# The loads of raw q and k go from SP's queue to GpSimd's in a fused attention and two-MoE kernel

## The chip, the cores and the metric

One core of a Trainium2 chip runs the whole program. The metric is the device time of one execution in microseconds (us), the median of several runs. Engines are named as in the profile: PE (TensorE), DVE (VectorE), ACT (ScalarE), POOL (GpSimd), SP (SyncE, which only issues DMAs here).

## The reference

Causal attention with a bias from a running sum, then two dense two-layer blocks on its output, all in float32:

```python
scores = scale * np.matmul(q, k.transpose(0, 1, 3, 2))        # B, H, S, D = 4, 8, 576, 64
cum = np.cumsum(np.maximum(s, 0.0), axis=-1)
bias = -(cum[:, :, :, None] - cum[:, :, None, :])
scores = np.where(causal, -1000000000.0, scores + np.minimum(bias, 0.0))
attn = softmax(scores)
x = np.matmul(attn, v)                                         # then [2304, 512]
h = np.maximum(x @ w_in, 0.0);  x = h * h @ w_out              # d_ff = 2048
h = x @ w_in2;                  out = h * np.cos(h) @ w_out2
```

## The kernel before, in words

**Work.** The 2304 tokens are cut into nine blocks of 256. `_units` lists 96 "heads": each is one head of one batch over a run of query rows (256, 192, 128 or 64 of them) of one block. A head is done in steps of up to 128 query rows, one "job" each; heads 24 to 31, 56 to 63 and 80 to 95 have one job, the others two. While the attention of later blocks runs, the first MoE block (lines 850 to 902: `g1`, `gact`, `grest`, `g2`) is done for earlier ones: each `step` (line 996) issues a part of the attention pipeline and one or more slots of 12 matmuls of `g1` (L857) or `g2` (L886). After about 535 us the attention is over; the rest of the first MoE block and then the second one (L1246, L1301) remain.

**One head, from 16 on.** `load_raw` (line 210) brings q and k transposed, 128 partitions by 448 to 768 floats, into a tile `raw` that has two buffers. `prep_high` (L347, L348 on ACT) casts it to float32r, `prep_low` (L355, L358 on DVE) subtracts and keeps the rest in the tiles `hi` and `k2`; L358 is the last reader of `raw`, so the load of head n+2 may start when L358 of head n has ended. `load_ext` (L340, issued by POOL) puts four rows of bias terms into `k2`; the buffer it writes is free when the last QK matmul (L502) of head n-2 has read it. Then come QK on PE (L502), mask and minimum on DVE (L516), exp on ACT (L533), two splits on DVE (L561, L565), a DMA transpose of the result issued by SP (L571), and PV on PE (L602). Where a job's width is no multiple of 128, POOL first clears the padding of the tile `p` (L560), and L561 of that job waits for it.

**Order of the work around the change.** Every engine and queue runs its instructions strictly in program order. In a head's first step, `heads_ahead` issues `load_ext` of the next head at the step's start, `prep_high` and `prep_low` of the next head in its middle, and at its very end `load_raw` of the head three further on:

```python
heads_ahead(i, (next_, load_ext, 2))
...
heads_ahead(i, (nhigh, prep_high, 2))
...
heads_ahead(i, (nlow, prep_low, 2))
...
heads_ahead(i, (nraw, load_raw, 4))
```

SP's queue holds, beside the raw loads, the weight loads (L179), the transposes (L571), the loads of prepared v (L368) and its stores (L433), and the stores of block results (L895). POOL's queue holds the ext loads (L340), the loads of v (L380) and the clearing of padding (L560).

Of the kernel before, what the change touches and what calls it, by code (L numbers as in the profile page):

```python
# [24 lines left out]
BT = 256  # L25
# [90 lines left out]
def attention_moe_moe_kernel(  # L116
# [18 lines left out]
    nc = tc.nc  # L135
# [74 lines left out]
    def load_raw(n):  # L210
        nq, nl = heads[n][6], heads[n][8]
        if n < H:
            return
        if n < EARLY:
            t = at.tile([128, KQ], F32, tag=("hi", "k2")[n % 2], bufs=2, name="early1")
            nc.sync.dma_start(out=t[0:64, 0:2 * BT], in_=qk[n, 0:64, 0:2 * BT])
            nc.sync.dma_start(out=t[64:66, 0:2 * BT], in_=c1_d[n - H])
            hd[n] = t
            return
        raw = at.tile([128, KQ], F32, tag="raw", bufs=2, name="raw")  # L220
        nc.sync.dma_start(out=raw[:, BT - nq:BT + nl], in_=qk[n, :, BT - nq:BT + nl])
        hd[n] = [None, None, raw]

    def v_own(b):
# [29 lines left out]
    def store_ones(eng, n0, n1):  # L254
# [10 lines left out]
        out=mask[:, 512:640], in_=mask[:, 512:640], pattern=[[-1, 128]], compare_op=ALU.is_ge,  # L265
# [4 lines left out]
        out=ident, in_=ident, pattern=[[-1, 128]], compare_op=ALU.not_equal, fill=1.0,  # L270
# [3 lines left out]
    for t in early[2:]:  # L274
        early_ones(t, nc.gpsimd)
    nc.vector.tensor_scalar(
        out=cs[0:32, 0:S], in0=cs[0:32, 0:S], scalar1=0.0, scalar2=8.0, op0=ALU.max, op1=ALU.mult
    )
    cc = []
    for x0, x1, t in ((0, BT, "xh"), (BT, S, "xl")):  # L280
        nc.vector.tensor_tensor_scan(
            out=c8[0:32, x0:x1], data0=cs[0:32, x0:x1], data1=cs[0:32, x0:x1],
# [713 lines left out]
    def step(moe=0, bits=0, attn=True):  # L996
# [52 lines left out]
        if attn:  # L1049
            heads_ahead(i, (nraw, load_raw, 4))  # L1050
# [104 lines left out]
    for k in range(NB1):  # L1155
# [8 lines left out]
        for i in range(J):  # L1164
# [24 lines left out]
            n = len(slots) - last - nslots + math.ceil(nslots * (i + 1) / J)  # L1189
# [233 lines left out]
```

## Time and profile before

| what | value |
|---|---|
| median of 3 runs | 1001.28 us (999.33 to 1001.86) |
| the profiled execution, its own time | 998.74 us |
| span of the profiled execution | 997.0 us |
| busy, share of the span | PE 96%, PEld 74%, DVE 73%, ACT 66%, POOL 16% |
| granted TensorE clock | 1.0 throughout |
| DMA queue of SP and ACT (q1) | 119.05 MB, 46.4% of 16 engines' span |
| DMA queue of POOL (q0) | 6.29 MB, 2.4% |

Busy shares are averages over stages with different limits. A busy PE is no PE at its peak, since matmuls overlap in the records; what counts is where PE stands idle and what ended the idle time. DMA issues are not counted as busy. The views used below are: the table of stretches, the chain of work that ended last, the waits (who waited for whom), the timeline, and the view of one line or tile.

### The profile page before, as it was taken

Reading aid. Unit: us, or ns where it says so; the run is one execution under the profiler, and the core shown is the slowest. Engines: PE = TensorE matmul, PEld = TensorE weight load, DVE = VectorE, ACT = ScalarE, POOL = GpSimd, SP = SyncE. Lnnn points to the kernel's source line nnn. Section 1 sums busy time; section 2 is a strip of 40 time slices with the busy share of each in tenths; the row PEclk is TensorE's granted clock in tenths of the full one; section 3 lists DMA queues with packets and bytes.
Section 4 is the critical chain, followed back from the end, with each engine's and each line's share of the span. In section 5 each row is a group of like instructions: output and inputs, shape, how many; then the busy total and the mean of one; then the engine's idle time right before and its main releaser. Section 6 shows DMA issues by size and latency. Waiting matters only on the chain.

```text
span 997.0 us, 20518 instructions
## 1 busy us (share of the span) xinstructions
PE 961.9 (96%) x7266; PEld 738.4 (74%) x7266; DVE 723.6 (73%) x1865; ACT 654.6 (66%) x1596; POOL 162.3 (16%) x258
## 2 busy tenths in 40 slices
PE   5999899999999999999999999999999999999998
PEld 4798898899999998999999997444544454444444
DVE  6879788878778897777987267798987545545555
ACT  5789776778778777676776587777865443433433
POOL 2000011111111111111210022430043340001101
PEclk9999999999999999999999999999999999999999
DMA  8955589756897876477898579110000000011001
GB/s 275 296 175 181 145 198 197 163 131 161 178 180 168 182 192 150 118 147 164 189 214 167 194 260 354 62 40 1 1 1 1 0 1 1 3 40 43 27 17 64
DMA packets 150711, 126.65 MB, mean 127 GB/s; under 512 B 108048, under 2 KB 125792, under 8 KB 150608
## 3 DMA queue, kind: packets, MB, share of 16 engines
q1 hardware_dynamic: 146688, 119.05, 46.4%
q0 software_dynamic: 3904, 6.29, 2.4%
q8 instruction: 57, 0.93, 0.4%
q14 instruction: 46, 0.38, 0.1%
q10 hardware_dynamic: 16, 0.01, 0.0%
HBM read 85.25 MB, written 15.81 MB: 101 GB/s over the span
## 4 chain that ended last, share of the span: by engine, by line
PE 81%; DVE 10%; ACT 5%; issue 2%; DMA 2%; SPq 0%; DVEq 0%; ACTq 0%
PE hps L857 19%; PE y L886 18%; PE o L1301 17%; PE hp L1246 17%; PE qkp L502 4%; PE pvs L602 4%; DVE wt L750 1%; DVE st L729 1%; DVE sb L516 1%; DMA raw<-in_qk_dram 1%; PE xps L657 1%; DVE wt L753 1%; PE qkp L493 1%; ACT st L719 1%; ACT sb L533 1%
## 5 line engine op out<-in xcount | busy, mean ns | idle before, releaser
L857 PE MATMUL hps<-xh,wt 128*128 128x256 f32 x1152 | 239.8, 291 | 4.2 <-ACT g L868 4.1
L886 PE MATMUL y<-gh,wt 128*128 128x256 f32 x1152 | 236.7, 289 | 0.0
L857 PEld LDWEIGHTS hps<-xh,wt 128*128 128x128 f32 x1152 | 190.3, 192 | 6.9 <-ACT g L868 5.8
L886 PEld LDWEIGHTS y<-gh,wt 128*128 128x128 f32 x1152 | 188.9, 191 | 1.2
L1246 PE MATMUL hp<-yh,wt 128*128 128x512 f16 (+1 forms) x640 | 185.9, 358 | 0.0
L1301 PE MATMUL o<-wt,gh 128*128 128x512 f16 x576 | 171.3, 379 | 2.0 <-ACT wt L1316 1.9
L886 PE MATMUL y<-gl,wt 128*128 128x256 f32 x576 | 163.0, 283 | 2.7 <-DVE gl L876 2.7
L857 PE MATMUL hps<-xl,wt 128*128 128x256 f32 x576 | 163.6, 284 | 0.9 <-DVE xl L674 0.9
L1246 PEld LDWEIGHTS <-wt 128*128 128x128 f16 x960 | 92.2, 98 | 93.3
L1258 ACT ACTIVATE a<-hp,hsc 128x512 f32<-128x512 f32 (+1 forms) x80 | 51.4, 643 | 118.2 <-PE hp L1246 116.8
L868 ACT ACTIVATE g<-hps 128x256 f32<-128x256 f32 x144 | 54.6, 379 | 106.4 <-PE hps L857 104.8
L1246 PE MATMUL hp<-yl,wt 128*128 128x512 f16 (+1 forms) x320 | 114.4, 358 | 0.0
L886 PEld LDWEIGHTS y<-gl,wt 128*128 128x128 f32 x576 | 110.1, 191 | 3.7 <-DVE gl L876 3.1
L857 PEld LDWEIGHTS hps<-xl,wt 128*128 128x128 f32 x576 | 111.0, 193 | 1.4 <-DVE xl L674 1.1
L1301 PE MATMUL o<-wt,gl 128*128 128x512 f16 x288 | 109.2, 379 | 0.4 <-DVE gl L1288 0.4
L1259 DVE TENSOR_SCALAR kf<-a 128x512 f32<-128x512 f32 (+1 forms) x80 | 33.6, 420 | 103.7 <-ACT a L1258 103.3
L1301 PEld LDWEIGHTS <-gh 128*128 128x128 f16 x576 | 56.2, 98 | 66.7 <-issue 2.4
L533 ACT ACTIVATE sb<-sb,nb 128x128 f32<-128x128 f32 (+8 forms) x160 | 93.7, 586 | 11.8 <-DVE nb L516 11.5
L340 POOL DMA_DIRECT2D k<-ext_d x80 | 40.9, 511 | 336.2 <-ACT g L869 94.9
L516 DVE CUSTOM_DVE_ANT_0 sb<-qkp,mask 128x128 f32<-128x128 f32 (+8 forms) x160 | 72.6, 454 | 12.5 <-PE qkp L493 5.5
L1267 ACT ACTIVATE a<-kf 128x512 f32<-128x512 f32 (+1 forms) x80 | 46.8, 585 | 46.9 <-DVE kf L1260 46.4
L876 DVE TENSOR_TENSOR gl<-g,gh 128x256 fp32r<-128x256 f32 x144 | 60.0, 417 | 21.5 <-PE y L886 10.4
(119 smaller groups left out, 1690.3 us busy)
## 6 DMA issues: line engine op xcount, KB each, us to landing
rw<-in_w_dram SPq DMA_DIRECT2D x64, 512.0 KB
raw<-in_qk_dram SPq DMA_DIRECT2D x32, 352.0 KB
raw<-in_qk_dram SPq DMA_DIRECT2D x16, 384.0 KB
v_d<-vt SPq DMA_DIRECT2D x16, 320.0 KB
raw<-in_qk_dram SPq DMA_DIRECT2D x16, 320.0 KB
vb<-v_d SPq DMA_DIRECT2D x32, 160.0 KB
vr<-in_v_dram POOLq DMA_DIRECT2D x15, 320.0 KB, 4.4
y_d<-yst SPq DMA_DIRECT2D x18, 256.0 KB
```

The costliest lines, as they stand in the source:

```text
L340: nc.gpsimd.dma_start(out=hd[n][1][64:68, BT - nq:BT + nl], in_=ext_d[n, :, BT - nq:BT + nl])
L502: nc.tensor.matmul(p[0:r, 0:cn], m[0:kk, qo:qo + r], m[0:kk, BT + c0:BT + c0 + cn], start=(kk == 128), stop=(kk == 68),)
L516: nc.vector.tensor_tensor_reduce(out=sb[0:r, c0:c0 + cn], in0=p[0:r, 0:cn], in1=mask[0:r, mo + c0:mo + c0 + cn], scale=-0.125, scalar=(3.0 ...
L533: nc.scalar.activation(out=sb[0:r, 0:w], in_=sb[0:r, 0:w], func=ACTF.Exp, scale=-1.0, bias=j["nb"], accum_out=pd[n - h % 2]["z"][0:r, ti, ...
L857: nc.tensor.matmul(hp, w[:, a, c * 128:(c + 1) * 128], (xh, xl)[e][:, c, :], start=(n == 0), stop=(n == 3 * KD - 1),)
L868: nc.scalar.activation(out=g, in_=hp, func=ACTF.Relu)
L876: nc.vector.tensor_tensor(out=gl, in0=g, in1=gh, op=ALU.subtract)
L886: nc.tensor.matmul(yps[k][d // 2][:, d % 2, :], w[:, a, d * 128:(d + 1) * 128], (gh, gl)[e], start=(f == 0 and n == 0 and d % 2 == 0), sto ...
L1246: nc.tensor.matmul(hp, w[:, a, c * 128:(c + 1) * 128], (yh, yl)[e][:, c, :], start=(m == 0), stop=(m == 3 * KD - 1),)
L1258: nc.scalar.activation(out=a, in_=hp, func=ACTF.Copy, scale=sm["hsc"][:, j, f:f + 1], bias=0.25)
L1267: nc.scalar.activation(out=a, in_=kf, func=ACTF.Sin, scale=-6.2831850)
L1301: nc.tensor.matmul(ops[j][a], (gh, gl)[e][:, a * 128:(a + 1) * 128], w[:, x, :], start=(first and m == 0), stop=(last and m == 2),)
```

## The change

The 80 loads of `raw` (heads 16 to 95) are issued by GpSimd instead of SP. Nothing else is changed; the loads of heads 8 to 15 (lines 216, 217) stay on SP.

```diff
         raw = at.tile([128, KQ], F32, tag="raw", bufs=2, name="raw")
-        nc.sync.dma_start(out=raw[:, BT - nq:BT + nl], in_=qk[n, :, BT - nq:BT + nl])
+        nc.gpsimd.dma_start(out=raw[:, BT - nq:BT + nl], in_=qk[n, :, BT - nq:BT + nl])
         hd[n] = [None, None, raw]
```

POOL, in the last stretch of one-job heads (`k_` with a number is the tile of one ext load; the first row is the ext load of head 90, the fourth that of head 91):

```order
 L340 DMA k_8593<-ext_d 4x704
 L560 MEMSET p 128x2x64
+L221 DMA raw<-in_qk_dram 128x704
 L340 DMA k_8673<-ext_d 4x704
 L560 MEMSET p 128x2x64
```

Between an ext load with its clearing and the next such pair there now stands one raw load: that of head 92 stands ahead of the ext load of head 91.

SP in the same stretch, before and then now:

```order
L221 DMA raw<-in_qk_dram 128x704
L571 DMA_TRANSPOSE pt<-p 128x10x128
L895 DMA y_d<-yst 128x512 x2
L368 DMA vb<-v_d 128x640
L221 DMA raw<-in_qk_dram 128x704
```

```order
L368 DMA vb<-v_d 128x640
L571 DMA_TRANSPOSE pt<-p 128x10x128
L895 DMA y_d<-yst 128x512 x2
L368 DMA vb<-v_d 128x640
L571 DMA_TRANSPOSE pt<-p 128x10x128
```

The raw load has left its place behind a transpose, two stores of block results and a load of v; nothing else on SP changed its order.

POOL at the program's start (`early` are tiles of the first heads, `vr` holds v):

```order
 L191 MEMSET early 2x2x256
 L192 MEMSET early 2x2x256
+L221 DMA raw<-in_qk_dram 128x768
 L380 DMA vr<-in_v_dram 128x2x320
+L221 DMA raw<-in_qk_dram 128x768
```

The first raw load (head 16) now follows the clearing at the start directly, ahead of POOL's first load of v; its buffer has no earlier user.

## Rows read from the trace of the kernel before

**Rows 1.** The page: busy time by engine, and the chain by engine.
```profile
PE 961.9 (96%) x7266; PEld 738.4 (74%) x7266; DVE 723.6 (73%) x1865; ACT 654.6 (66%) x1596; POOL 162.3 (16%) x258
...
PE 81%; DVE 10%; ACT 5%; issue 2%; DMA 2%; SPq 0%; DVEq 0%; ACTq 0%
```

**Rows 2.** Stretches: length, busy PE, PEld, DVE, ACT, POOL, clock, DMA share, GB/s.
```profile
0.00:40.00 40.00, 29.06 (x111) 24.12 (x112) 31.42 (x96) 24.43 (x68) 5.95 (x15) 1.00 0.87 285
...
165.00:210.00 45.00, 40.54 (x408) 36.79 (x408) 35.27 (x117) 30.94 (x92) 8.39 (x20) 1.00 0.75 177
...
500.00:535.00 35.00, 33.61 (x359) 32.93 (x358) 30.81 (x88) 25.16 (x65) 5.44 (x16) 1.00 0.90 204
```

**Rows 3.** Chain in order of time (start, length, what): its pieces on raw.
```profile
166.74 4.20 DMA raw<-in_qk_dram
...
512.06 4.26 DMA raw<-in_qk_dram
```

**Rows 4.** Waits, 78 to 540 us: who waited for whom; total us, times, longest.
```profile
ACT hi L347 <- DMA raw<-in_qk_dram: 15.6, 12, 4.6
...
DVE hi L355 <- ACT hi L347: 5.7, 12, 1.2
...
DVE p L561 <- POOL p L560: 8.4, 10, 1.1
...
PE hps L857 <- ACT g L868: 2.9, 5, 1.0
...
PE qkp L502 <- DVE hi L355: 0.7, 1, 0.7
```

**Rows 5.** Timeline around the raw load of head 91: start, length, what, [idle before].
```profile
507.34 0.75 DVE L358 TENSOR_TENSOR k<-raw,hi 64x576 fp32r<-64x576 f32 x1
...
508.48 1.94 SPq L571 DMA_TRANSPOSE pt<-p  x1
...
510.47 1.05 SPq L895 DMA_DIRECT2D y_d<-yst  x2
...
512.06 0.43 SPq L221 DMA_DIRECT2D raw<-in_qk_dram  x1
...
516.40 0.78 ACT L347 CAST hi<-raw 128x704 fp32r<-128x704 f32 x1 [2.03 <-DMA raw<-in_qk_dram]
...
517.71 0.38 PE L857 MATMUL hps<-xh,wt 128*128 128x256 f32 x1 [0.72 <-ACT g L868]
```

**Rows 6.** View of L340: issue (ns min/median/max) and landing of the ext loads.
```profile
L340 POOL DMA_DIRECT2D k<-ext_d x80: 502/508/729, 75.7 to 528.5; - x80
...
DMA to landing us min/median/max: 1.8/3.2/5.9
```

**Rows 7.** View of L380: landing of POOL's loads of v.
```profile
DMA to landing us min/median/max: 3.3/4.4/6.4
```

**Rows 8.** Timeline around the ext load of head 91, POOL, DVE and PE.
```profile
510.97 0.50 POOL L340 DMA_DIRECT2D k<-ext_d  x1 [3.22 <-DVE p L561]
...
511.46 0.22 POOL L560 MEMSET p<- 128x128 f16 x1
...
512.58 0.75 DVE L358 TENSOR_TENSOR k<-raw,hi 64x576 fp32r<-64x576 f32 x1
...
514.46 0.46 DVE L561 TENSOR_SCALAR p<-sb 128x576 f16<-128x576 f32 x1
...
519.37 0.29 PE L502 MATMUL qkp<-k 68*128 68x288 f32 x1
```

**Rows 9.** Timeline of POOL at the start: its first load of v.
```profile
74.46 0.76 POOL L380 DMA_DIRECT2D vr<-in_v_dram  x1 [67.73 <-ACT wt L738]
```

**Rows 10.** Timeline: L561 beside a load that POOL issues, and alone.
```profile
164.99 0.75 POOL L380 DMA_DIRECT2D vr<-in_v_dram  x1 [2.68 <-PE qkp L502]
...
165.35 0.64 DVE L561 TENSOR_SCALAR p<-sb 64x576 f16<-64x576 f32 x1
...
169.44 0.45 DVE L561 TENSOR_SCALAR p<-sb 64x576 f16<-64x576 f32 x1
```

## The prediction

> **What bounds the kernel now.** I read the page first. PE is busy for 96% of the span and holds 81% of the chain [rows 1]; the time can only fall where PE stands idle or waits. The table of stretches then says where the moved loads matter. They lie between 78 and 540 us, and the two stretches with most of PE's trouble there are 165 to 210, with 40.54 busy of 45, and 500 to 535, with 33.61 of 35 [rows 2]. In both, heads have a single job, so a raw load is due every four to five microseconds. DVE is close behind PE there: 30.81 of 35. The clock is 1.00 throughout, so it is no part of the sum.
>
> Next the chain in order of time, because a wait counts only if it is on it. Raw loads are on it twice, for 4.20 and 4.26 us, in just these two stretches [rows 3]. The waits say how much arrives at PE. ACT waits for raw 12 times, 15.6 us in all; DVE waits behind that cast for 5.7 us; but PE's own idle time behind ACT's L868 is 2.9 us and behind DVE's L355 it is 0.7 us [rows 4]. Most of ACT's waiting is slack that PE never sees.
>
> The timeline shows why a load is late. L358 of head 89 starts at 507.34, takes 0.75 and so frees the buffer at 508.09. SP is then at a transpose (508.48, 1.94 us) and two stores (510.47, 1.05), and issues the load at 512.06, 3.97 us after it could have. ACT gets the data at 516.40, 4.34 us after the issue, having been idle for 2.03; PE loses 0.72 just after [rows 5]. The load itself is not slow, its place in the queue is.
>
> **The change part by part.** It removes 80 DMAs from SP, adds 80 to POOL, and moves each past other work on both.
>
> *Earlier issue.* On POOL, a raw load stands behind an ext load and a clearing that were released before L358 ended, so it goes at 508.1 instead of 512.1. Its landing from POOL's queue is not in the trace. From below it is bounded by the ext loads, median 3.2 us [rows 6], from above by the slowest load of v, 6.4; I take the median of the loads of v, 4.4 [rows 7], since those are 320 KB and a raw load is 352 in this stretch. That gives 512.5. ACT was ready at 516.40 - 2.03 = 514.37, so this wait goes, and it nearly goes even at 6.4 (514.5). What PE can win is its idle time behind these waits, 2.9 + 0.7 = 3.6 us at most [rows 4], and nothing at least, if another wait is due at once. DVE is next there: it has 35 - 30.81 = 4.2 us of idle time in 35. I take -2.5 us, two thirds, because the five waits behind L868 are not all behind a raw load.
>
> *The ext load, now behind the raw load.* Each raw load stands ahead of the next head's ext load and waits for DVE. Before, the ext load of head 91 went at 510.97; the L358 of head 90 that the raw load ahead of it needs ends at 512.58 + 0.75 = 513.33 [rows 8]. Add the raw load's own issue, which lies between 0.51 for 4 rows [rows 6] and 0.75 for a load of v [rows 10]; I take 0.75, the nearer in size. So the ext load goes at 514.1, 3.1 us later than before. With its median of 3.2 us it lands at 517.3, and if it can't land before the raw load ahead of it in the same queue, at 513.33 + 4.4 = 517.7. QK needs it at 519.37 [rows 8]. That is 1.7 us of cover; at the slowest landing, 5.9 [rows 6], it would be 0.6 late. I take +0.3 us in all. One late landing in ten of the 32 one-job heads would be 3 x 0.6 = 1.8, which is the bound. Heads with two jobs have a whole further step between the raw load and the next ext load; there I take nothing.
>
> *The clearing, now behind both.* The clearing after the ext load then ends at 514.08 + 0.50 + 0.22 = 514.80, while the L561 that needs it ran at 514.46 [rows 8]: 0.34 us of new waiting on DVE. It comes in every second one-job head, since after each pair DVE has the division of the pair's output between, which covers it: 16 x 0.34 = 5.4 us of DVE time. Such waits exist already, 8.4 us of them [rows 4], and PE is busy all the same. What hides them is DVE's idle time, 4.2 in 35, about 0.5 us a head, more than 0.34 in every second one. I take +0.6, with 0 and 5.4 as bounds.
>
> *The start.* POOL does nothing from 74.46 - 67.73 = 6.73 us until its load of v [rows 9]. The raw load of head 16 has nothing to wait for and so is issued at 6.7 instead of 78. In the first 40 us the DMA engines are 87% busy and move 285 GB/s [rows 2]; 128 x 768 x 4 bytes = 393 KB at that rate take 1.4 us. If weights and first heads come later by all of it, that is +1.4; if the remaining 13% take it, nothing. I take +0.4.
>
> *DVE beside POOL's issues.* L561 took 0.64 us beside a load issued by POOL and 0.45 without one [rows 10]. A raw load's issue starts where L358 ends and is over 0.75 later, while the next L561 comes 514.46 - 513.33 = 1.13 after it [rows 8]. I take 0; if every load hit such an instruction, it would be 80 x 0.19 = 15 us of DVE time, hidden in part. The trace shows how weakly the other side is disturbed: 80 ext loads took 502 to 729 ns to issue, with a median of 508, while DVE was busy for 73% of the span [rows 6, 1].
>
> *SP.* It loses 80 issues and what they waited for. Its transposes still wait for their own inputs and for free buffers; I take 0, and no loss, since none of its work is put behind anything new.
>
> **Sum.** -2.5 + 0.3 + 0.6 + 0.4 + 0 + 0 = -1.2 us against the profiled execution's 998.74, that is 997.5. The median of the runs shown, 1001.28, is 2.5 above that execution, so on its scale the forecast is **1000.1 us**. A measurement of this kernel can tell about 0.3%, 3 us, from no change; the forecast is no measurable difference.
>
> **Rivals.**
>
> *A: the raw waits were worth more than PE's idle time shows.* For it: the chain holds 8.46 us of raw loads [rows 3], and ACT and DVE wait 15.6 and 5.7 us [rows 4]; freed, they run ahead and take other small waits from PE. Against it: PE is 96% busy, and its recorded idle time behind these waits is 3.6. If half of the 8.46 comes out and nothing is given back, the time is about 997; if all does, 993.
>
> *B: POOL's line becomes the loop, and it is slower.* L358 of one head, then the raw load's issue, the ext load's, the clearing, L561, and from there DVE's work up to the next L358. Place: the 32 one-job heads. Price: 5.4 us of clearing, 1.8 of ext loads, 1.4 at the start, with 0.5 of the gain left, so +8.1 and 1009 in full, 1005 when half of it gets through. It decides where DVE's idle time, 0.5 us a head, no longer covers the wait: at a raw issue of about 1.4 us instead of 0.75. For it: DVE is at 88% in that stretch. Against it: the gain removes DVE's own 5.7 us of waiting behind the cast, which is as much as the clearing costs.
>
> *C: DVE holds up POOL's issues.* As a mechanism here: a raw issue that has to sit out one DVE instruction of 0.75 us [rows 8] makes the load, the ext load and the clearing behind it that much later: 32 x 0.75 = 24 us of further DVE waiting, of which 32 x 0.5 = 16 is covered, so some +8 on top of B, 1015. The Trainium skill, page "SBUF — State Buffer", section "SBUF: two separate sides", states it as a rule against this change: a DMA issued from GpSimd has its descriptors written through a port that some VectorE instructions hold for themselves, and the page's advice is to issue from SP or ACT. By its figure (section "A bandwidth-pool intuition that's wrong", 3100 ns against 620) an estimate is 2.5 us more for each load. The trace doesn't bear it out: no ext load took over 729 ns to issue [rows 6].
>
> That the loads are not moved is excluded: the order shows all 80 on POOL.
>
> **Chances.** Forecast 0.49; A 0.23; B 0.24; C 0.04. Faster by over 0.3% (under 998.3) is A, 0.23; within 0.3%, 0.49; slower (over 1004.3) is B and C, 0.28. **Range** 996.0 to 1006.5: downwards the full 3.6 and the runs' own spread (999.33 to 1001.86), which leaves out the last tenth with A's 993; upwards most of B, leaving out its full price and C.
>
> **What would show it.** Right: ACT's wait for raw falls from 15.6 us to under 5; raw loads go within 0.3 us of L358's end; POOL's landing of raw is 4 to 5 us; the chain has no raw in it; waits of L561 for L560 grow by several us; PE's busy share stays near 96%. Wrong: PE waits for an ext load at L502 (B by the ext load), DVE's idle time in 500 to 535 used up and PE's busy time there below 33 (B by the clearing), or raw issues of over 1 us on POOL (C). If PE's waits behind L868 and L355 go and the time falls by more than 3 us, the sum undervalued the chain (A).

## The result and the profile after

The changed kernel takes **1010.49 us** (median of 6 runs, 1008.17 to 1016.9) against 1000.49 (6 runs, 998.35 to 1001.86) for the kernel before on the same chip: ratio 1.0111, 95% interval 1.0081 to 1.0141. It is slower; the forecast was 1000.1 and no difference, the range ended at 1006.5. The profiled execution is the slowest of the six, 1016.9 us, with a span of 1015.1; another profile of the same kernel, called `again` below, has 1008.39 and 1006.6.

The page of the profile after, busy time and DMA queues, against [rows 1]:

```profile
PE 969.0 (95%) x7266; PEld 745.6 (73%) x7266; DVE 723.9 (71%) x1865; ACT 655.4 (65%) x1596; POOL 211.1 (21%) x338
...
q1 hardware_dynamic: 135168, 92.31, 37.3%
q0 software_dynamic: 10048, 33.03, 12.0%
```

The loads went where the change says: 26.7 MB have moved from SP's queue to POOL's, and DVE and ACT are as busy as before. The stretches, against [rows 2]:

```profile
0.00:40.00 40.00, 27.29 (x104) 22.53 (x104) 29.65 (x91) 23.40 (x64) 6.46 (x16) 1.00 0.88 286
165.00:210.00 45.00, 40.60 (x409) 37.95 (x410) 36.18 (x116) 31.53 (x92) 13.46 (x31) 0.96 0.73 168
310.00:360.00 50.00, 46.41 (x462) 45.19 (x460) 39.63 (x107) 37.16 (x100) 9.61 (x17) 0.99 0.98 176
...
500.00:535.00 35.00, 31.44 (x328) 30.64 (x327) 28.77 (x80) 25.48 (x64) 9.95 (x23) 1.00 0.93 202
```

In the last stretch of one-job heads PE has lost 2.17 us of 35 (33.61 to 31.44), and DVE has lost 2.04 too: it is not DVE that has become the bound, both wait. (The kernel is some 14 us behind by then, so this window holds earlier heads of the same stretch than it did before.) The clock column is the second thing to see: 0.96 and 0.99, where the kernel before had 1.00. The waits from 78 to 560 us (the last L502 now stands at 554.8, before at 536.1), against [rows 4]:

```profile
DVE p L561 <- POOL p L560: 11.5, 15, 1.3
...
ACT hi L347 <- DMA raw<-in_qk_dram: 11.0, 8, 2.1
...
PE qkp L502 <- DMA k<-ext_d: 9.3, 6, 3.9
...
DVE hi L355 <- ACT hi L347: 3.9, 9, 1.2
...
PE hps L857 <- ACT g L868: 0.5, 1, 0.5
```

ACT's waits behind raw fell from 15.6 to 11.0 us, and PE's own wait behind L868 went from 2.9 to 0.5. One wait is new, and it is PE's: L502 for the ext load. The views of L340 and L221 tell how late these loads are, against [rows 6] (this profile tells the landing of 73 of the 80 ext loads and 69 of the 80 raw loads):

```profile
L340 POOL DMA_DIRECT2D k<-ext_d x80: 521/522/817, 78.4 to 543.1; - x80
DMA to landing us min/median/max: 1.9/3.8/8.1
```

```profile
L221 POOL DMA_DIRECT2D raw<-in_qk_dram x80: 548/565/605, 6.7 to 541.1; - x80
DMA to landing us min/median/max: 3.0/4.1/9.5
```

A raw load now goes 0.55 us after the end of L358 in one-job heads (median; before 1.92), and the ext load behind it 1.11 us after, where it went 1.85 us ahead of that end before: it is 3 us later.

How one such load stops PE is seen in `again` at head 58, the third of the second one-job stretch. First the kernel before, the ext load of that head and the first matmul that needs it:

```profile
344.57 0.52 POOL L340 DMA_DIRECT2D k<-ext_d  x1 [0.70 <-PE qkp L502]
...
351.31 0.30 PE L502 MATMUL qkp<-k 68*64 68x288 f32 x1
```

And `again`, the timeline of the same head:

```profile
345.66 0.75 DVE L358 TENSOR_TENSOR k<-raw,hi 64x576 fp32r<-64x576 f32 x1
...
346.96 0.56 POOL L221 DMA_DIRECT2D raw<-in_qk_dram  x1 [2.67 <-ACT g L868]
...
347.52 0.52 POOL L340 DMA_DIRECT2D k<-ext_d  x1
...
351.65 0.30 PE L502 MATMUL qkp<-hi 128*64 128x288 f32 x1
...
355.20 0.47 PE L502 MATMUL qkp<-k 68*64 68x288 f32 x1 [3.25 <-ACT k L348]
```

The raw load of head 59 waits for L358 of head 57 (end at 346.41), the ext load of head 58 stands behind it and lands 7.54 us after its issue, at 355.06; 0.14 us later PE goes on, after 3.25 us of idle time. (The row puts the wait down to L348; that of head 58 had ended at 348.97.) The raw load of head 59, just ahead in the queue, took 7.32 us to land itself. The clock falls at 354.02, while PE still stands, and PE, busy for most of the next stretch, works at half speed (the column after the busy times is the granted clock; 0.50 is the 1.2 GHz level):

```profile
354.10:360.80 6.70, 5.60 (x34) 5.54 (x35) 1.86 (x6) 2.86 (x8) 1.29 (x3) 0.50 0.49 126
```

### The profile page after: what moved, and what is told of

Same layout as the page of the kernel before. It is cut to its first block, busy times and chain, and to the rows that moved or that the text cites. A ratio compares the mean times of both kernels' runs of the same rounds, so it can differ in the third digit from the quotient of the medians.

```text
span 1015.1 us, 20456 instructions
## 1 busy us (share of the span) xinstructions
PE 969.0 (95%) x7266; PEld 745.6 (73%) x7266; DVE 723.9 (71%) x1865; ACT 655.4 (65%) x1596; POOL 211.1 (21%) x338
## 4 chain that ended last, share of the span: by engine, by line
PE 42%; DVE 4%; ACT 2%; issue 1%; DMA 1%; DVEq 0%; POOL 0%; ACTq 0%; POOLq 0%
PE o L1301 17%; PE hp L1246 16%; PE y L886 4%; PE hps L857 4%; DMA k<-ext_d 1%; DMA raw<-in_qk_dram 1%; PE pvs L602 1%; ACT wt L744 0%; DVE kf L1260 0%; DVE wt L753 0%; DVE a L1273 0%; PE qkp L502 0%; DVE wsc L783 0%; DVE kf L1259 0%; ACT a L1258 0%
## 5 line engine op out<-in xcount | busy, mean ns | idle before, releaser
L886 PE MATMUL y<-gh,wt 128*128 128x256 f32 x1152 | 239.5, 291 | 0.0
L857 PEld LDWEIGHTS hps<-xh,wt 128*128 128x128 f32 x1152 | 192.4, 194 | 3.5 <-ACT g L868 2.4
L886 PEld LDWEIGHTS y<-gh,wt 128*128 128x128 f32 x1152 | 191.2, 193 | 1.2
L868 ACT ACTIVATE g<-hps 128x256 f32<-128x256 f32 x144 | 54.6, 380 | 124.6 <-PE hps L857 123.1
L221 POOL DMA_DIRECT2D raw<-in_qk_dram x80 | 45.4, 568 | 285.0 <-ACT gh L870 89.1
L561 DVE TENSOR_SCALAR p<-sb 128x512 f16<-128x512 f32 (+7 forms) x128 | 46.9, 367 | 44.4 <-ACT sb L533 16.6
L1267 ACT ACTIVATE a<-kf 128x512 f32<-128x512 f32 (+1 forms) x80 | 46.8, 585 | 46.9 <-DVE kf L1260 46.4
```

Of the source, the lines that this page charges most:

```text
L221: nc.gpsimd.dma_start(out=raw[:, BT - nq:BT + nl], in_=qk[n, :, BT - nq:BT + nl])
L561: nc.vector.tensor_scalar(out=p[0:r, 0:w], in0=sb[0:r, 0:w], scalar1=PSC, scalar2=None, op0=ALU.mult)
L857: nc.tensor.matmul(hp, w[:, a, c * 128:(c + 1) * 128], (xh, xl)[e][:, c, :], start=(n == 0), stop=(n == 3 * KD - 1),)
L868: nc.scalar.activation(out=g, in_=hp, func=ACTF.Relu)
L886: nc.tensor.matmul(yps[k][d // 2][:, d % 2, :], w[:, a, d * 128:(d + 1) * 128], (gh, gl)[e], start=(f == 0 and n == 0 and d % 2 == 0), sto ...
L1267: nc.scalar.activation(out=a, in_=kf, func=ACTF.Sin, scale=-6.2831850)
```

## The experiments

The theories, as they stood before the first runs: 1, the ext load waits behind a raw load that waits for L358, PE waits for it, and the clock falls behind the stall; 2, the two loads disturb each other in POOL's queue, whatever their order; 3, the clearing L560 is late; 4, the start. Theory 5, on the price of the clock, came later. All kernels were timed beside the kernel before. "L502 idle" is PE's idle time before L502's matmuls on `k` from 78 to 560 us, and "half clock" the time between 40 and 560 us at the 1.2 GHz level, both in the kernel's profile, whose span is the last column.

| kernel | median us | ratio to before, 95% interval | L502 idle | half clock | span |
|---|---|---|---|---|---|
| before | 999.0 to 1000.49 | | 0.6 | 0 | 997.0 |
| the change | 1010.49 | 1.0111 (1.0081 to 1.0141) | 13.7 | 20.5 | 1015.1 |
| `again`, the same | 1009.51 | 1.009 (1.007 to 1.0109) | 9.6 | 10.2 | 1006.6 |
| `ext_first` | 1001.04 | 1.0017 (0.9998 to 1.0037) | 0.6 | 3.4 | 1001.9 |
| `raw_last` | 1000.85 | 1.0008 (0.9992 to 1.0023) | 0.6 | 6.8 | 999.9 |
| `wait_only` | 1000.98 | 1.0007 (0.9995 to 1.002) | 2.0 | 6.8 | 1001.9 |
| `half_bytes` | 1009.36 | 1.0086 (1.0056 to 1.0116) | 7.3 | 10.2 | 1007.7 |
| `clear_first` | 1008.73 | 1.009 (1.0059 to 1.012) | 8.9 | 3.4 | 1003.1 |
| `start_sp` | 1012.45 | 1.0125 (1.009 to 1.016) | 12.4 | 13.6 | 1010.7 |
| `one_job_sp` | 999.22 | 0.9995 (0.9979 to 1.0011) | 0.6 | 6.8 | 999.8 |
| `longer_wait` | 1009.17 | 1.0098 (1.0078 to 1.0117) | 8.9 | 10.2 | 1009.9 |
| `one_stall` | 1004.01 | 1.0043 (1.0027 to 1.0059) | 3.6 | 3.4 | 999.8 |
| `one_job_last` | 1001.92 | 1.0021 (1.0 to 1.0042) | 0.9 | 6.8 | 1001.4 |
| `four_rows` | 1099.48 | 1.1023 (1.0987 to 1.106) | | | 1096.1 |

The column of idle time sorts the kernels: all with 7 us or more are slower by 0.86% to 1.25%, all with 2 or less by 0.21% at most.

**`again`: the change once more.**

> The change once more, for a profile that is not its slowest execution. All theories: 1007 to 1012 us, ratio 1.007 to 1.012. Theory 1 (the ext load waits behind a raw load that waits for L358, so QK waits for it at L502, and TensorE's granted clock falls for 3.41 us after such a stall): waits of L502 for the ext load of 5 to 10 us again, and fewer stretches at the 1.2 GHz level than the five of the 1016.9 us execution, each right behind a stall of PE; the difference between this profile and that one is their clock. If the time is as long with no stretch at half clock, the clock is no part of it.

Measured 1009.51. L502's idle time is 9.6 us, and there are two stretches at half clock instead of five, one of 3.41 us at 57.06 and one of 6.83 at 354.02, which begins in the stall shown above. The one at 57.06 stands behind no stall of L502. The span is 8.5 us shorter than that of the first profile, with 4.1 less idle time at L502 and 10.2 less at half clock. The group of matmuls, idle time last:

```profile
L502 PE MATMUL qkp<-k 68*128 68x288 f32 (+7 forms) x160 | 50.7, 322 | 9.6 <-DMA k<-ext_d 4.7 <-ACT k L348 3.3 <-DVE p L565 1.3
```

**`ext_first` and `raw_last`: the order on POOL.** Both keep every raw load on POOL. The first issues it just behind the next ext load, the second behind the clearing as well (`heads_ahead(i, (nraw, load_raw, 3))` after `softmax_tail` instead):

```diff
-            heads_ahead(i, (next_, load_ext, 2))
+            heads_ahead(i, (next_, load_ext, 2), (nraw, load_raw, 3))
...
-            heads_ahead(i, (nraw, load_raw, 4))
+            if job(i) and jobs[i][1] == 0:
+                upto(nraw, min(jobs[i][0] + 4, EARLY), load_raw)
```

> The raw load stays on GpSimd but is issued behind the next ext load instead of ahead of it. Theory 1 (order): the ext load lands as early as before the change, L502 waits for it under 1.5 us, no dip of the clock follows, and what is left is the start, some 2.4 us: 999 to 1004. Theory 2 (the two loads disturb each other in GpSimd's DMA queue, whatever their order): the same bytes are in the same queue, so 1007 to 1011 again with ext landings of up to 8 us. Theory 3 (the clearing L560 behind the loads): the clearing still stands behind a raw load, so DVE's L561 waits for it as long as with the change, 10 us or more, and 3 to 5 us of the loss stay: 1004 to 1007.

> The raw load stays on GpSimd, behind both the ext load and the clearing of the step. Theory 1: as with ext_first, 999 to 1004. Theory 3 (clearing): 3 to 5 us less than ext_first, and L561 waits for L560 no longer than before the change (8.4 us). Theory 2 (shared queue): 1007 to 1011.

Measured 1001.04 and 1000.85: the loss is gone with the same bytes in the same queue, so theory 2 falls. L502's idle time is what it was before the change:

```profile
L502 PE MATMUL qkp<-k 68*128 68x288 f32 (+7 forms) x160 | 50.0, 317 | 0.6 <-issue 0.5
```

Theory 3's figure missed too: in `ext_first` L561 waits only 0.4 us for L560, in `raw_last` 8.0, and the times are the same.

**`wait_only`: the wait without the load.** The kernel before, with this after each raw load on SP:

```diff
+        if n >= EARLY + 2:
+            k2 = hd[n - 2][1]
+            scr = at.tile([1, 1], F32, tag="scr", bufs=1, name="scr")
+            nc.gpsimd.tensor_copy(out=scr, in_=k2[0:1, BT:BT + 1])
+            for _ in range(4):
+                nc.gpsimd.memset(scr, 0.0)
```

> The kernel before, raw loads on SP, but at the place where the change issues them on GpSimd a copy of one element that L358 wrote and four 1-element clearings stand (some 0.5 us together): the wait without the load. Theory 1: the ext loads go 2.5 to 3 us later than before, L502 waits for them 4 to 9 us, some dips of the clock: 1004 to 1009. Theory 2 (shared queue): nothing is added to the queue, so as before, 1000 to 1002. If it is as before although the ext loads are issued as late as with the change, lateness of issue alone does not cost, and the raw bytes ahead of them do.

Measured 1000.98: a miss for theory 1 as it stood. The ext loads of one-job heads go 1.29 us after L358's end, later than with the change, and L502 waits 2.0 us in all. But they land in 3.1 us (median of one-job heads), and with the change in 4.2. In `again`, an ext load issued within 0.8 us behind a raw load landed 0.15 to 1.72 us after it, never before (40 cases). So I changed the theory: what counts is when the ext load lands, and it takes both, the late issue and the load ahead of it that it does not overtake.

**`half_bytes`, `clear_first`, `start_sp`, `one_job_sp`: size, clearing, start and place.** The edits: rows 64 to 127 of each raw load back on SP; the clearing ahead of raw and ext load (`load_ext` split in two, its DMA issued after `softmax_tail` behind the raw load); head 16's raw load on SP; and

```diff
-        nc.gpsimd.dma_start(out=raw[:, BT - nq:BT + nl], in_=qk[n, :, BT - nq:BT + nl])
+        eng = nc.sync if 26 <= n < 34 or 58 <= n < 66 or n >= 82 else nc.gpsimd
+        eng.dma_start(out=raw[:, BT - nq:BT + nl], in_=qk[n, :, BT - nq:BT + nl])
```

> Rows 0 to 63 of a raw load stay on GpSimd, ahead of the ext load and waiting for L358 as with the change; rows 64 to 127 go back to SP. So the ext load is as late as in the change and in wait_only, with half the bytes just ahead of it. Theory 1b (after the first runs: it takes both, the late issue and the raw bytes just ahead in the queue): between wait_only and the change, 1002 to 1007, median landing of the ext loads in one-job heads between 3.1 and 4.2 us. Theory 2b (any raw load ahead of the ext load costs the same, whatever its size): 1008 to 1011. If half the bytes cost nothing, 999 to 1002, the price sets in only with a full load ahead.

> All raw loads on GpSimd and still just ahead of the next ext load, but the clearing L560 of the step now goes ahead of both. Theory 1b: the ext load still lies late and behind the raw bytes, so 1007 to 1012 as with the change. Theory 3 (clearing): the loss goes, 999 to 1003, with L561 waiting under 3 us for L560.

> The change, but the first raw load, head 16's, is back on SP, so nothing of it runs at 6 us. Theory 4 (the start costs up to 2.4 us, as the slowest profile has it): 1006 to 1008, 2 us less than the change. Theory 1b (the start cost of that profile is one stretch at half clock, which comes in profiles without an early raw load too): 1008 to 1011, within 1 us of the change.

> The change for the other heads alone: the 30 raw loads that stand ahead of an ext load in the one-job stretches (heads 26 to 33, 58 to 65, 82 to 95) are back on SP. Theory 1b: in heads with two jobs the ext load has a whole further step, so nothing is lost there, and all of the loss goes: 999 to 1002. If loads of two-job heads cost as well, 1003 to 1007.

Half the bytes cost as much as all, 1009.36, a miss for the theory as just changed, which had 1002 to 1007: half a raw load lands hardly sooner (median 3.7 us against 4.0 in `again`), and the ext load behind it lands in 4.2 again. (ACT also waits 27.5 us for raw there, as its other half comes from SP late; that part of the time is not separated.) With the clearing out of the way, L561's waits for it fall to 2.7 us, and the time stays at 1008.73: theory 3 falls. Without the early load at 6 us the time is 1012.45, no lower (and above the 1008 to 1011 expected of theory 1b): theory 4 falls. Of the 2.4 us by which the first profile was behind at 64 us, 1.3 came with a stretch at half clock at 58.48; `wait_only`, with nothing changed there, was 2.2 behind. And with the 30 loads ahead of ext loads in one-job stretches back on SP it is 999.22: the whole loss sits there, as the prediction had placed it.

**`longer_wait` and `one_stall`: lateness alone, and one stall alone.** Both are the kernel before with raw on SP. `hold` stands ahead of the ext load, and the clearing ahead of both; in `longer_wait` its condition is `n >= EARLY + 2` and the number 12:

```diff
+    def hold(n):
+        if n == 59:
+            scr = at.tile([1, 1], F32, tag="scr", bufs=1, name="scr")
+            nc.gpsimd.tensor_copy(out=scr, in_=hd[n - 2][1][0:1, BT:BT + 1])
+            for _ in range(28):
+                nc.gpsimd.memset(scr, 0.0)
...
+            heads_ahead(i, (nwait, hold, 3), (nextd, fill_ext, 2))
```

> Raw loads on SP as before; ahead of each ext load a copy of one element that L358 wrote and twelve 1-element clearings, some 1 us more than in wait_only, so the ext load lands as late behind L358 as with the change (5.3 us in one-job heads) with no load ahead of it; the clearing L560 goes ahead of them, as in clear_first. Theory 1c (only the time of landing counts, and the last microsecond of it decides): 1005 to 1011, L502 waiting for the ext load 4 to 10 us. Theory 2c (it takes a load ahead in the queue): 999 to 1003.

> The kernel before with one ext load made late, head 58's, the one at whose L502 PE stood longest with the change (3.25 us): on GpSimd a copy of one element that L358 of head 57 wrote and 28 one-element clearings go ahead of it, some 3.9 us. Theory 5 (after such a stall TensorE's granted clock falls to 1.2 GHz for 3.4 or 6.8 us, and that costs half of it again): one stall of 2.5 to 4 us at 350 to 358 us, a stretch at half clock within 5 us behind it, and 1003 to 1007 in all, 1.5 to 3.5 us more than the stall. Without theory 5: no such stretch there, and 1002 to 1004, the stall alone.

`longer_wait`, without one raw load on POOL, is as slow as the change, 1009.17. Its ext loads go 2.71 us after L358's end and land in 3.0, so at 5.7; with the change it is 1.11 and 4.2, at 5.3; in `wait_only` 1.29 and 3.1, at 4.4, and that was free. So lateness alone makes such a loss, and about the last microsecond of it decides. Its idle time before L502 (here L514):

```profile
L514 PE MATMUL qkp<-k 68*128 68x288 f32 (+7 forms) x160 | 50.5, 321 | 8.9 <-DMA k<-ext_d 6.4 <-DVE gl L888 1.8 <-ACT sb L545 0.5
```

`one_stall` made one ext load late (the timeline, where L352 is the ext load), and the stretch behind it ran at half clock:

```profile
345.45 4.23 POOL L346 MEMSET scr<- 1x1 f32 x28
...
350.06 0.52 POOL L352 DMA_DIRECT2D k<-ext_d  x1 [0.37 <-issue]
...
353.63 0.32 PE L514 MATMUL qkp<-k 68*64 68x288 f32 x1 [3.05 <-DMA k<-ext_d]
```

```profile
354.40:357.70 3.30, 3.30 (x26) 3.24 (x25) 0.56 (x4) 1.02 (x3) 0.71 (x2) 0.50 0.01 3
```

The L876 that stands at 344.54 us in the kernel before comes 0.84 us sooner in this profile, the one at 383.37 comes 3.80 later: the stall of 3.05 has cost 4.64, so 1.6 us come from the 3.41 us at half clock (354.33 to 357.74). Its ten runs took 1000.41 to 1006.95, ratio 1.0043: one late ext load of 80 makes 0.4 to 0.5 of the change's loss. (In this kernel all ext loads and clearings stand at another place of the step too, and no run has that alone; up to the stall its profile was no slower than that of the kernel before.)

**`four_rows`.** Rows 0 to 3 on POOL, the other 124 on SP.

> Of each raw load only rows 0 to 3 stay on GpSimd ahead of the ext load and waiting for L358; the other 124 rows go back to SP. Theory 1c (the ext load lands just behind the load ahead of it in its queue, whatever that one's size; half a raw load landed in 4.15 us, a whole one in 4.2): if four rows land as an ext load does, in 3.1 to 3.3 us, the ext load lands some 0.7 us earlier than with the change, and the time is nearer to wait_only: 1000 to 1004. Theory 2c (any load just ahead costs as much as a whole one): ext landing in one-job heads of 4.0 or more and 1007 to 1011.

Measured 1099.48, no answer to the question: something else became slow. SP's queue takes 58.4% of the DMA engines' time for 118.21 MB, where it took 46.4% for 119.05:

```profile
q1 hardware_dynamic: 145408, 118.21, 58.4%
```

and between 500 and 535 us three pairs of SP's transposes take 4.81 to 5.88 us, where single ones took 1.32 to 2.35 before. The Trainium skill, page "DMA: Bandwidth & Descriptors", section "Why a DMA increments its semaphore by 16 and not by 1", says that a DMA runs on the largest number of engines up to 16 that divides its row count; 124 rows would run on 4 where 128 run on 16. The trace agrees as far as it goes (more engine time for fewer bytes); no run here tells the engines apart.

**`one_job_last`: the gain without the price?** The converse of `one_job_sp`, each of the 30 loads behind the ext load and the clearing:

```diff
+    def on_pool(n):
+        return 26 <= n < 34 or 58 <= n < 66 or n >= 82
...
+    def raws(i, d, late):
+        if job(i) and jobs[i][1] == 0:
+            while nraw[0] < min(jobs[i][0] + d, NH) and (late or not on_pool(nraw[0])):
+                load_raw(nraw[0])
+                nraw[0] += 1
```

> The 30 raw loads of the one-job stretches alone on GpSimd (the converse of one_job_sp), each behind the ext load and the clearing of its step, the other 50 on SP as before: the gain of the change without its price. If the raw loads' earlier issue is worth the 2.5 us of the prediction: 996 to 998, ratio 0.997 to 0.999. If, as ext_first and raw_last have it, PE gets 0.4 to 0.8 us out of it between 500 and 540 and next to nothing elsewhere, because loads from GpSimd's queue come 0.9 us later behind their issue than SP's: 998 to 1000, ratio 0.998 to 1.001, no difference that can be told.

Measured 1001.92, no gain, and above both expectations. Its profile gained 1.3 us on the kernel before in the first one-job stretch (162 to 180 us), lost 1.0 in the second, and lost 4.4 at 515 to 529, this time by a raw load:

```profile
514.57 0.57 POOL L225 DMA_DIRECT2D raw<-in_qk_dram  x1 [2.16 <-ACT sb L537]
...
523.43 0.78 ACT L351 CAST hi<-raw 128x704 fp32r<-128x704 f32 x1 [4.76 <-DMA raw<-in_qk_dram]
...
524.74 0.58 PE L867 MATMUL hps<-xh,wt 128*128 128x256 f32 x1 [3.48 <-ACT g L878]
```

It landed 8.84 us after its issue, PE stood for 3.48, and the clock was at half from 523.88 for 6.83 us. In the kernel before, the 12 raw loads that ACT waited for took 2.95 to 4.64 us from SP's issue to the cast, 4.27 in the median; the 14 of `raw_last` took 4.05 to 10.61 from POOL's issue, median 5.80, and the 12 of `ext_first` 5.80 as well. So a load that goes 1.4 us earlier behind L358 and is 1.5 us longer on its way gains nothing. That holds for loads that ACT waited for; the trace has landings for POOL's loads alone, so it is not shown that loads from SP never take 9 us, nor the "0.9 us later" of my expectation for all loads.

## Why the prediction was wrong

**The ext load is the step that failed.** The prediction had the mechanism (the raw load ahead waits for L358, the ext load behind it can't land sooner, PE waits at L502) and the place, and took +0.3 us with 1.8 as the bound, from "1.7 us of cover" at head 91 and 0.6 of lateness at the slowest landing. The profiles show 9.0 (`again`) and 13.1 (after) more idle time before L502. Three parts of the term were too small. The raw load goes 0.55 us after L358's end and not at once, and its issue takes 0.57 (0.75 was taken): the ext load goes 1.11 us after that end, not 0.77 (514.1 less 513.33). The landing was priced by the ext load's own median and slowest, 3.2 and 5.9, while in one-job heads it is 4.2 behind the raw load, and up to 8.1; raw loads themselves took up to 9.5, over the 6.4 that was to bound them. And the cover of one head stood for all 32, and that head had more than most. Before, head 91's ext load landed 2.9 us after its issue at 510.97, so 5.5 us ahead of its L502 at 519.37 [rows 8]:

```profile
DMA to landing us min/median/max: 2.9/2.9/2.9
```

Of the 32 one-job heads only three had more; the median was 3.85, the least 1.03. An issue 3 us later and a landing 1 us longer use up 3.85. In `again` the median is 0.79, and in 13 of the 32 heads the load landed under 0.3 us ahead of L502, which is where PE waits for it. So it was not one head in ten: a usual one-job head had hardly any cover left, and each slow landing became idle time of PE.

**"The clock is 1.00 throughout, so it is no part of the sum" failed too.** It was so in the one profile that was read. Of the 25 executions of the kernel before that were timed beside `again`, 12 had a mean granted clock of 0.996 to 0.998, and took 1000.9 us in the median against 998.7 for the other 13. In the first 78 us `wait_only` is the kernel before, and there a stretch of 3.41 us at half clock cost 1.34 (the same L876 is 0.88 us late ahead of it and 2.22 behind it); in `one_stall` it was 1.6. With 0.43 us for each microsecond, the mean of the two, the change's profile lost 8.8 us to the clock and `again` 4.4. The Trainium skill, page "TensorE: Matmul & The Clock Gate", section "HAM oscillation — how this bites in real kernels", describes the chain, a wait for a DMA that lets the clock fall, with half of the throttled time as the price; `one_stall` agrees, with 0.47, and `wait_only` has 0.39.

Not all of this is the change's. Stretches near 57 to 60 and 117 to 120 us come in profiles without the change as well (`wait_only`, `one_job_sp`), behind waits that the kernel before has too, at full clock. Here is the second of these waits, in the kernel before, then in the change's profile with the stretch that follows it only there:

```profile
116.41 0.38 PE L399 MATMUL xps<-ss,ones 128*128 128x2 f32 x2 [1.55 <-ACT vt L391]
```

```profile
119.24 0.38 PE L399 MATMUL xps<-ss,ones 128*128 128x2 f32 x2 [1.55 <-ACT vt L391]
```

```profile
119.90:123.30 3.40, 3.40 (x16) 3.21 (x15) 0.98 (x3) 1.17 (x3) 0.13 (x1) 0.50 0.18 74
```

They hold 6.8 of the 20.5 us in the change's profile and 3.4 of the 10.2 in `again`. The other 13.7 and 6.8 us stand at stalls of L502 and cost 5.9 and 2.9 by the same price. Why a wait of this length is followed by half clock in one execution and not in another is open.

With all the clock in, the terms come to 13.1 + 8.8 = 21.9 against 18.1 on the span for the change, and 9.0 + 4.4 = 13.4 against 9.6 for `again`: 3.8 us too much in both.

**The gain that was predicted stands in the idle time, but early raw loads alone do not make it.** Predicted were 2.5 of at most 3.6 us. From 78 to 560 us, PE's idle time before everything but L502's matmuls on `k` fell from 12.3 us to 8.6 (after) and 8.8 (`again`), near the 3.8 left over above (`clear_first` and `start_sp` have 8.7 and 8.8); PE's wait behind L868 fell from 2.9 to 0.5 and the one behind L355 from 0.7 to 0 and 0.4. ACT's wait for raw did not fall under 5 but to 11.0 (12.1 in `again`), raw loads went 0.55 us after L358 instead of 0.3, and their landing was 4.1, in the 4 to 5 of the sign. What makes the gain is open: `ext_first`, `raw_last` and `one_job_last` issue raw loads of one-job heads as early, have next to no stalls at L502, and have 15.3, 12.0 and 13.3 us of that idle time and no gain in time; `longer_wait` has the stalls, its raw loads on SP, and 12.4.

**The small terms.** The clearing, +0.6: its waits grew from 8.4 to 11.5 us as predicted and cost nothing that `clear_first` could give back. The start, +0.4: nothing that `start_sp` could give back. DVE beside POOL's issues, 0: right, in the two profiles of the change no raw load took over 0.605 us to issue, so rival C falls. SP, 0: nothing speaks against it, with no raw load on SP `ext_first` takes 0.17% more, with an interval that reaches 0.9998.

**Rival B** came nearest with 1009 in full, by the wrong parts: 5.4 of clearing, which cost nothing, 1.4 of the start, which neither, and 1.8 of ext loads, where idle time and the clock behind it took 12 to 19. Its sign, a wait of L502 for the ext load, is what the profile shows; DVE's idle time was not used up. **Rival A** asked for raw waits worth more than PE's idle time; no kernel that frees them was faster.

## What to carry to other kernels

In a queue that runs in order, a transfer that waits makes every transfer behind it late. Put the one with the nearest deadline first: exchanging two calls here took back the loss. Price such a step head by head: the cover that each head has, less the later issue, against the landings of the load ahead, slow ones among them. One place, or one median, is not enough. Count a stall of TensorE at up to one and a half times its length, since the clock can fall with it (4.64 us for 3.05 in `one_stall`); whether it falls differs between executions of one kernel, so one profile at full clock does not take it out of the sum.

## What was not expected of the hardware

Loads of POOL's queue landed in the order of their issue, as far as the traces tell their landing: in the profiles of the change (two), `half_bytes`, `clear_first`, `start_sp`, `ext_first`, `raw_last` and `one_job_sp` none of 1194 neighbouring pairs issued within 6 us of each other landed in the other order. Half of the bytes of such a load landed hardly sooner (3.7 against 4.0 us). In `one_stall` PE's clock fell 0.70 us after the end of a stall of 3.05 us and was at 1.2 GHz for 3.41; in `again` it fell 2.07 us into a stall of 3.25 and stayed there for 6.83.
